# Attention and a rational feed-forward block on one core: a shared step one place later, one normalisation and one block moved, two transfers cut in two

## The chip, the cores and the metric

The kernel runs on one NeuronCore of a Trainium2 chip. The metric is the device time of one execution in microseconds (us). Engines are named as in the profile: PE is TensorE (matmuls; PEld its weight loads), DVE is VectorE, ACT is ScalarE, POOL is GpSimd, SP is the engine that issues nearly all transfers here.

## The reference, cut to what matters

Attention over 4 batches, 8 heads, 576 positions and 64 dimensions, with a bias made by a small network from the distance of two positions, followed by a feed-forward block whose activation is a quotient of polynomials:

```python
scores = (q @ k.T) / 8 + bias            # bias[h,i,j] = relu(x*w1 + b1) @ w2
                                         # x = log1p(|i-j|) / log1p(max(i,1))
attn   = softmax(scores); x = attn @ v   # x: 2304 tokens x 512
h = x @ w_in                             # 512 -> 2048
P = a0 + a1*h + a2*h^2 + a3*h^3
Q = 1 + |b0|*|h| + |b1|*h^2
out = (P / (Q + 1e-6)) @ w_out           # 2048 -> 512
```

All is float32; the feed-forward matmuls are split into a high and a low part (three products for one).

## The kernel before, in words

**Three stages.** First a table of the bias is made, in 36 blocks of 16 rows (lines 688 to 788). For each block four `relu` rows are made on DVE or ACT (line 725), PE multiplies them by the small weights (line 761), ACT scales the result into a tile `e` (line 767), and SP writes it to a table in DRAM (line 772), from which bias tiles are read back (`load_bias`, line 252). Then comes attention, 72 steps taken two at a time in rounds (`rnd`, line 590). Then the feed-forward block, in two passes of 20 steps each (lines 954 to 1001).

**Steps of attention.** A unit `u` is a pair of heads and a batch; there are 16. A unit has 576 rows of scores: four steps of 128 rows (`c` = 0 to 3), and 64 rows that are left. The remainders of units `u` and `u+1` go together as one shared step, written `(u, 4)` with `u` even. Two units make a group of nine steps (`steps`, lines 321 to 323): `(u,0) ... (u,4), (u+1,0) ... (u+1,3)`. Nine is odd and a round takes two steps, so in even groups the shared step is the first of its round, and in odd groups the second. An ordinary step's scores are made with weights in tiles of 64 by 128, a shared step's with tiles of 64 by 64 (line 341); the transposes of line 425 use 64 by 128 and the products with `v` (line 484) 128 by 64.

**A round.** On PE: the scores of steps `i` and `i+1`, the transposes of the probabilities of `i-2` and `i-1`, the products with `v` of `i-3` and `i-2`. On DVE: the bias and the row minimum (`e_ttr`, line 357), copies out of PSUM, and a part of the conversion of the feed-forward weights. On ACT: the exponentials (line 373) and the copies of the transposes (line 440).

**The division by the row sums.** When a unit's last step has been transposed, its sums go through DRAM: `put_tails` writes them (`rs<-rt`, line 462), and `load_rb` (line 386) reads them back, spread over the partitions, with four transfers (`rb<-rs`, lines 392 and 396). `e_norm` (line 401) multiplies the unit's output by them, on POOL (line 408; for unit 12 and the last on DVE), and its result is stored (line 410). Where these are placed is written out in `done_to` (line 530): `load_rb(2g)` at place `7 - g % 2` of group `g`, the normalisation of unit `2g` after the first step of the next group. `rnd` puts at most one normalisation into a round, in a free place of POOL: in the slot `pool`, or in `pool2`.

**The weights.** A job of conversion takes its weights through three rounds (`job_plan`, line 560): POOL copies the middle bits (`wm<-wx`, line 177), DVE joins them (line 181, list `between`), POOL subtracts (line 188, slot `pool2`). In the rounds 11, 20 and 29 the slot `pool` is free: there POOL runs the normalisation of units 2, 6 and 10, then that round's subtraction, then the next round's `wm` copy, for which DVE's join of the next round waits.

**SP's queue.** SP issues in the written order, and an issue that waits holds all behind it. Its issues of a round of the code go out about two rounds of PE later here. The order that the rounds 26 and 27 give is now: the six pieces of a bias load, `rs` of unit 10, `ws<-wl`, `wx` (weights for round 29), `ws<-wh`, `rb` of unit 10 (four), `v`, `q`, `k`, `xr` (the first load of tokens), `ws<-wl`, `wx`. The sizes follow from the tiles: `q` and `k` 288 KB each, `v` 320, `wx` 512, `ws` or `wih`/`woh` 256, this `xr` 576, `rb` 288 in all, `rs` 5.

Of the kernel before, what the change touches and what calls it, by code (L numbers as in the profile page):

```python
# [12 lines left out]
AF = mybir.ActivationFunctionType  # L13
ALU = mybir.AluOpType
# [3 lines left out]
P = 128  # L18
# [3 lines left out]
DM, DFF, NT = 512, 2048, B * S  # L22
# [7 lines left out]
NTT = len(TS)  # L30
# [7 lines left out]
def tile_attn_moe(  # L38
# [194 lines left out]
    with tc.manual_schedule():  # L233
# [3 lines left out]
        with ExitStack() as actx:  # L237
# [82 lines left out]

            steps = [(0, 0), (0, 1), (0, 2), (1, 0), (1, 1), (0, 3), (0, 4), (1, 2), (1, 3)]
            for u in range(2, len(units), 2):
                steps += [(u, c) for c in range(5)] + [(u + 1, c) for c in range(4)]
            s2, prob, pt, tl, xs = {}, {}, {}, {}, {}
            rsum, rb = {}, {}

# [182 lines left out]

            def loads(i):  # L510
                g, c = divmod(i, UPG)
                for u, x, y in ((2 * g + 2, 0 if g else 4, 3 if g else 6), (2 * g + 3, 5 if g else 7, 8)):
                    if u < NU and c == x:
                        load_qk(u)
                    if u < NU and c == y and u != 3:
                        load_v(u)
                if i == UPG + 1:
                    load_v(3)
                p, r = divmod(i, 2 * UPG)
                r = {2: 0, 7: 1, 11: 2, 13: 3, 16: 4}.get(r)  # L520
                if r is not None and p + 1 < NP:
                    load_bias(p + 1, r)
                if i == NS - 18:
                    load_x(0, 0, 0, KD - 1)
                if i == NS - 5:
                    load_x(1, 1, 0, KD - 1)
# [3 lines left out]
            def done_to(k):  # L530
                g, c = divmod(k, UPG)
                u = 2 * g - 2
                if g > 0:
                    if c == (0 if g > 1 else 1) and u != NX or k == NS:
                        norms.extend(e_norm(u))
                    if c == 6 and g * 2 < NU:
                        norms.extend(e_norm(u + 1))
                    if c == 2 and u + 1 < NU - 1:
                        load_rb(u + 1)
                if k == NS - 8:  # L540
                    x12.append(xs[NX])
                    late.extend(e_norm(NX))
                if g < NU // 2 and c == (7 - g % 2 if g else 8):
                    load_rb(2 * g)

            def run(todo):
                while todo:
                    todo.pop(0)()
# [41 lines left out]
            def rnd(r):  # L590
                i = 2 * r
                plan = job_plan(r)
                loads(i)
                op = None
                while puts:
                    op = puts.pop(0)()
                for x in plan["first"]:
                    op = x()
                for x in plan["act"]:
                    x()  # L600
                us = ended(i - 4, i - 3)
                sa, sb = e_qk(i), e_qk(i + 1)
                b, o = side(i), side(i + 1)
                ZZ = (o + 1, o + 3)
                main, ends, adds, copy = e_tp(i - 2, (b, b + 1), ZZ, us)
                main_, ends_, _, copy_ = e_tp(i - 1, (b + 2, b + 3), ZZ)
                weave(sa[0] + sb[0], sa[1] + sb[1])
                for k in ("pool", "pool2"):
                    if not plan[k] and norms:
                        plan[k].append(norms.pop(0))  # L610
                        break
                for x in plan["pool"]:
                    x = x()
                    if op is not None:
                        behind(x, op)
                e_ttr(i, 0, True)
                op = e_ttr(i, 1)
                for x in plan["between"]:
                    op = x()
                for x in plan["pool2"]:  # L620
                    behind(x(), op)
                small = [ends[r] + ends_[r] + adds[r] for r in range(2)]
                weave(main[0][:4] + small[0] + main[0][4:] + main_[0], main[1] + small[1] + main_[1])
                copy(1, 2)
                copy(0, 1)
                copy_(0, 2)
                for j in range(2):
                    e_ttr(i + 1, j)
                put_tails(i - 2, 2, ZZ, us)
                put = e_pv(i - 3, b + 1) if i > 2 else None  # L630
                puts.append(e_pv(i - 2, b))
                hi = split_x(0, (i - NS + 12) // 2) if i in (NS - 12, NS - 10, NS - 8) else ()
                if i == NS - 4:
                    hi = split_x(0, KD - 1, x12[0][:, :TS[0]])
                for x in hi[:1]:
                    x()
                for k in (i, i + 1):
                    for j in range(2):
                        e_exp(k, j)
                recip(i - 2)  # L640
                recip(i - 1)
                if put:
                    put()
                for x in plan["last"] + list(hi[1:]):
                    x()
                done_to(i - 2)
                done_to(i - 1)
                run(late)
                loads(i + 1)
                if r == 2:  # L650
                    for x in jobs[:3]:
                        x[0]()
# [35 lines left out]
            with ExitStack() as bctx:  # L688
# [6 lines left out]
                lts = tpool.tile([P, S], F32, tag="lts", name="lts")  # L695
                bts = tpool.tile([P, NG * 4], F32, tag="bts", name="bts")
                LCUT = 320
                nc.scalar.dma_start(out=cs, in_=cst)
                nc.sync.dma_start(out=lts[:, :LCUT], in_=ltab[:, :LCUT])
                nc.sync.dma_start(out=lts[:, LCUT:], in_=ltab[:, LCUT:])  # L700
                for u in range(2):
                    load_qk(u)
                load_v(0)
                G.memset(qc, 1.0 + 1e-6)
                G.memset(wmin, -8.0 * 0x38000000)
                V.tensor_scalar(out=bts, in0=pts, scalar1=b1s, scalar2=None, op0=ALU.mult)
                A.activation(out=w28, in_=cs[:, 8 + 5 * NG:], func=AF.Identity, scale=8.0)
                for a, z in ((0, LCUT), (LCUT, S)):
                    V.tensor_scalar(
                        out=lts[:, a:z], in0=lts[:, a:z], scalar1=w1s, scalar2=None, op0=ALU.mult  # L710
# [34 lines left out]
                for y, n in enumerate(order):  # L745
                    if y == 13:
                        load_v(1)
                    if y + LEAD < NG:
                        relu(order[y + LEAD])
                    i0 = NROW * n  # L750
                    mid = i0 + NROW - 1
                    pa = 2 * ((y if y >= NG - 2 else y + 2) % 4)
                    pa = (pa, pa + 1)
                    cuts = sorted({0, mid, 512, EW})
                    for a, z in zip(cuts, cuts[1:]):
                        b = pa[a // 512]
                        o = W[:, b, a % 512:a % 512 + z - a]
                        for c in range(4):
                            x = rows[n, c]
                            x = x[:, a - mid:z - mid] if a >= mid else x[:, mid - a:mid - z:-1]  # L760
                            on(T.matmul(  # L761
                                o[32 * c:32 * c + 32], w28[:, 32 * c:32 * c + 32], x,
                                start=True, stop=True,
                            ), b)
                    e = rpool.tile([P, EW], F32, tag="e", name=f"e{n}")
                    o = 512 * pa[0]
                    on(A.activation(  # L767
                        out=e, in_=WF[:, o:o + EW], func=AF.Identity, scale=rts[:, n:n + 1]
                    ), *pa)
                    g, k = divmod(n, 8)  # L770
                    x0 = S - NROW - i0
                    nc.sync.dma_start(
                        out=tab[g][NROW * k:NROW * k + NROW, :, x0:x0 + EW].rearrange("r h x -> (r h) x"),
                        in_=e,
                    )
                    if y in done:
                        load_bias(0, done[y])
                    if y == NG - 1:
                        load_bias(0, 3)
                        load_bias(0, 4)  # L780
                    if y == NG - 3:
                        start(0)
                    if y == NG - 1:
                        start(1)
                        for k in range(2):
                            for j in range(2):
                                e_exp(k, j)
# [19 lines left out]
        with ExitStack() as mctx:  # L807
# [111 lines left out]
            def evac(ready):  # L919
                for n, c in ready:  # L920
# [5 lines left out]
                        part[t, c] = dpool.tile([P, DM], F32, tag=f"pa{t}_{c}", name=f"pa{t}_{c}")  # L926
                        nc.sync.dma_start(out=part[t, c], in_=o)
                    else:
                        o = pre.pop((t, c))
                        on(V.tensor_tensor(out=o, in0=po.pop((n, c)), in1=o, op=ALU.add), OB[c], mem="o")  # L930
                        nc.sync.dma_start(out=out[r0:r0 + P, :], in_=o)

            def load_part(t):
                for c in range(TS[t] // P):
# [145 lines left out]
```

## Time and profile before

| what | us |
|---|---|
| median of 3 runs | 661.66 (660.95 to 662.17) |
| the profiled execution's own time | 662.25 |
| its span, first to last instruction | 660.5 |
| PE busy | 653.5 (99%) |
| DVE busy | 561.3 (85%) |
| ACT busy | 472.2 (71%) |
| POOL busy | 154.1 (23%) |

The table of the bias takes the first 49 us or so, attention lasts to about 265 us, the feed-forward block to the end. Busy shares are of the whole span; a matmul's end is modelled, so PE's rounds are best read from the starts of their first instructions. Rounds are numbered as in the code: round 6 starts at 79.72 us, round 29 at 214.31 us.

### The profile page before, as it was taken

How to read it: one execution, taken by the hardware profiler on the slowest of the kernel's cores; microseconds unless marked ns; L12 is line 12 of the kernel's file. 1: busy time of each engine (PE TensorE's matmuls, PEld its weight loads, DVE VectorE, ACT ScalarE, POOL GpSimd, SP SyncE). 2: the span in 40 equal slices, each digit the busy share in tenths (PEclk: the TensorE clock that was granted, in tenths of full speed). 3: DMA queues.
4: the chain of work that ended last, by engine and by line, in shares of the span. 5: the costliest groups of instructions: out<-in, count | busy, mean ns of one | idle time of the engine just before them, and what ended most of it. 6: DMA issues, size and time to landing. Idle time of an engine off the chain costs nothing.

```text
span 660.5 us, 16193 instructions
## 1 busy us (share of the span) xinstructions
PE 653.5 (99%) x6274; PEld 546.8 (83%) x6274; DVE 561.3 (85%) x1100; ACT 472.2 (71%) x758; POOL 154.1 (23%) x108
## 2 busy tenths in 40 slices
PE   9999999999999999999999999999999999999997
PEld 6657888888888878988888888989988888888996
DVE  7997889988988895899999989979769779687776
ACT  7988999999999987767667566576656555555551
POOL 0000233333433330122212121222221221212211
PEclk9999999999999999999999999999999999999999
DMA  7887878868987975452825607669431301312031
GB/s 242 294 310 226 273 240 266 259 228 231 321 277 226 330 238 167 156 187 72 264 97 164 229 21 249 214 207 318 146 111 49 129 0 65 110 42 86 1 113 48
DMA packets 74845, 118.98 MB, mean 180 GB/s; under 512 B 11904, under 2 KB 33808, under 8 KB 74768
## 3 DMA queue, kind: packets, MB, share of 16 engines
q1 hardware_dynamic: 74624, 117.79, 54.2%
q8 instruction: 49, 0.80, 0.5%
q14 instruction: 28, 0.23, 0.1%
q10 hardware_dynamic: 144, 0.16, 0.1%
HBM read 79.17 MB, written 35.61 MB: 174 GB/s over the span
## 4 chain that ended last, share of the span: by engine, by line
PE 96%; DMA 1%; ACT 1%; issue 1%; DVE 0%; SPq 0%; POOL 0%; DVEq 0%; ACTq 0%; POOLq 0%
PE ps L316 30%; PE ps L909 30%; PE ps L484 12%; PE ps L341 11%; PE ps L761 6%; PE ps L425 6%; DMA tab<-e 1%; DMA bias<-tab 1%; PE ps L713 1%; ACT pt L440 1%; ACT p L373 1%; DVE s L357 0%; SPq L260 0%; DVE pre L930 0%; ACT wh L165 0%
## 5 line engine op out<-in xcount | busy, mean ns | idle before, releaser
L879 POOL TENSOR_TENSOR gl<-m,r 128x1024 fp32r<-128x1024 f32 (+1 forms) x39 | 85.6, 2195 | 295.5 <-DVE m L872 255.7
L830 ACT ACTIVATE w<-ps,babs 128x1024 f32<-128x1024 f32 (+1 forms) x40 | 41.3, 1033 | 107.1 <-PE ps L316 103.4
L373 ACT ACTIVATE p<-s,m 128x576 f32<-128x576 f32 x144 | 110.5, 783 | 0.2 <-DVE m L357 0.2
L357 DVE CUSTOM_DVE_ANT_0 s<-ps,bias 128x576 f32<-128x576 f32 (+1 forms) x144 | 95.2, 682 | 10.1 <-PE ps L341 3.9
L440 ACT COPY pt<-ps 128x512 f32<-128x512 f32 (+1 forms) x109 | 71.9, 732 | 17.6 <-PE ps L425 17.0
L909 PE MATMUL ps<-wol,gh 128*128 128x512 f32 x216 | 84.2, 390 | 0.0
L909 PE MATMUL ps<-woh,gh 128*128 128x512 f32 x216 | 84.2, 390 | 0.0
L341 PE MATMUL ps<-k,q 64*128 64x288 f32 (+1 forms) x640 | 82.3, 418 | 0.4 <-ACT e L767 0.2
L842 DVE SCALAR_TENSOR_TENSOR u<-w,babs,ps 128x1024 f32<-128x1024 f32 (+1 forms) x40 | 46.9, 1172 | 38.1 <-ACT t L831 38.0
L484 PE MATMUL ps<-pt,v 128*64 128x128 f32 (+1 forms) x1280 | 78.2, 265 | 0.8 <-ACT pt L440 0.5
L484 PEld LDWEIGHTS ps<-pt,v 128*64 128x64 f32 x1280 | 65.1, 137 | 5.8 <-ACT pt L440 1.6
L316 PE MATMUL ps<-xb,wih 128*128 128x512 f32 (+1 forms) x240 | 68.8, 367 | 0.0
L341 PEld LDWEIGHTS ps<-k,q 64*128 64x128 f32 (+1 forms) x640 | 50.9, 175 | 20.8 <-issue 6.4
L837 ACT ACTIVATE u<-u 128x1024 f32<-128x1024 f32 (+1 forms) x40 | 39.1, 978 | 40.2 <-DVE u L842 40.0
L425 PEld LDWEIGHTS ps<-ident,p 64*128 64x128 f32 x1296 | 49.6, 138 | 8.7 <-DVE m L357 2.9
L858 DVE SCALAR_TENSOR_TENSOR gh<-t,cst,r 128x1024 fp32r<-128x1024 f32 (+1 forms) x40 | 47.0, 1174 | 9.3 <-ACT r L839 6.9
L909 PE MATMUL ps<-woh,gl 128*128 128x512 f32 x216 | 53.8, 389 | 0.0
L425 PE MATMUL ps<-ident,p 64*128 64x64 f32 x1296 | 51.8, 226 | 0.5 <-ACT p L373 0.2
L865 DVE SCALAR_TENSOR_TENSOR m<-u,qc,gh 128x1024 f32<-128x1024 f32 (+1 forms) x40 | 47.1, 1178 | 4.0
L316 PEld LDWEIGHTS ps<-xb,wih 128*128 128x128 f32 x240 | 44.5, 188 | 6.1
L872 DVE SCALAR_TENSOR_TENSOR m<-t,cst,m 128x1024 f32<-128x1024 f32 (+1 forms) x40 | 47.1, 1179 | 1.4
L851 DVE SCALAR_TENSOR_TENSOR t<-t,cst,ps 128x1024 f32<-128x1024 f32 (+1 forms) x40 | 47.0, 1175 | 1.4
(82 smaller groups left out, 1343.9 us busy)
## 6 DMA issues: line engine op xcount, KB each, us to landing
tab<-e SPq DMA_DIRECT2D x36, 295.5 KB, 3.5
wx<-in_w_in_dram SPq DMA_DIRECT2D x16, 512.0 KB, 5.4
wx<-in_w_out_dram SPq DMA_DIRECT2D x16, 512.0 KB, 4.2
v<-in_vp_dram SPq DMA_DIRECT2D x16, 320.0 KB, 6.3
ws<-wh SPq DMA_DIRECT2D x20, 256.0 KB, 4.7
ws<-wl SPq DMA_DIRECT2D x20, 256.0 KB, 4.3
q<-in_qt_dram SPq DMA_DIRECT2D x16, 288.0 KB, 4.1
k<-in_kt_dram SPq DMA_DIRECT2D x16, 288.0 KB, 3.3
```

The source lines that it names most:

```text
L316: on(T.matmul(hps[s][:, j, :w_], w[:, k, sl], x[:, k, :w_], start=(k == 0 and z == 0), stop=(k == KD - 1 and z == 2),), b + j)
L341: on(T.matmul(W[o, b, :SH], q[r, x], k[r, a * SH:(a + 1) * SH], start=True, stop=True), b)
L357: op = on(V.tensor_tensor_reduce(out=t3[:, a], in0=W[:, b:b + 2][:, a, :SH], in1=b3[:, a], scale=-0.125, scalar=least, op0=ALU.add, op1=AL ...
L373: A.activation(out=prob[i][:, z * S:z * S + S], in_=t, func=AF.Exp, bias=m, scale=-1.0, accum_out=sums[u % 4][:, k:k + 1],)
L425: on(T.transpose(W[:, b, o:o + 64], src[x, :], ident[x, x]), b)
L440: on(A.copy(out=t.rearrange("p x (r s) -> p r x s", r=2)[:, a:z], in_=W[:, to[a]:to[a] + z - a].rearrange("p r (x s) -> p r x s", s=64),), ...
L484: on(T.matmul(ps[y, o], vt[n][:, kc, y], w_, start=(kc == 0), stop=(kc == 4)), b, mem=(f"pt{i % 3}", f"tl{i // 2 % 2}"))
L851: on(V.scalar_tensor_tensor(out=rt[s, "t"], in0=rt[s, "t"], scalar=abs_[:, 1:2], in1=hp(s), op0=ALU.add, op1=ALU.mult,), *hb(s), mem="t")
L865: V.scalar_tensor_tensor(out=m, in0=rt[s, "u"], scalar=qc, in1=rt[s, "gh"].bitcast(F32), op0=ALU.add, op1=ALU.mult,)
L872: V.scalar_tensor_tensor(out=m, in0=rt[s, "t"], scalar=abs_[:, 0:1], in1=m, op0=ALU.add, op1=ALU.subtract)
L879: eng.tensor_tensor(out=lo, in0=rt[s, "m"], in1=rt[s, "r0"], op=ALU.mult)
L909: on(T.matmul(po[n, c], l[:, j, c * P:(c + 1) * P], r[fp][:, j, :], start=(first and x is a), stop=(last and x is z),), OB[c])
```

## The change

The shared step of groups 1, 3 and 5 goes one place later, behind the first step of unit `u+1`, so that it is the first of its round there as well. What hangs on its place moves along: unit `u` ends one step later, so its sums are written one round later (`rs`, by the rule that writes a unit's sums when its last step has been transposed), `load_rb(2g)` in these groups goes one place later, which is one round later, and so does the load of `q` and `k` of unit `2g+3`, from the start to the end of a round. The normalisation of unit `2g` keeps its place. The normalisation of unit 12 goes from the end of round 33 to the middle of round 34, on DVE. The last block of the bias table is scaled on DVE. The constants are loaded in two pieces, the second holding the weights `w2`. The last tile of the output is added and stored in two halves of its columns.

```diff
             for u in range(2, len(units), 2):
-                steps += [(u, c) for c in range(5)] + [(u + 1, c) for c in range(4)]
+                if u % 4 and u + 2 < len(units):
+                    steps += [(u, c) for c in range(4)] + [(u + 1, 0), (u, 4)]
+                    steps += [(u + 1, c) for c in range(1, 4)]
+                else:
+                    steps += [(u, c) for c in range(5)] + [(u + 1, c) for c in range(4)]
...
-                for u, x, y in ((2 * g + 2, 0 if g else 4, 3 if g else 6), (2 * g + 3, 5 if g else 7, 8)):
+                for u, x, y in ((2 * g + 2, 0 if g else 4, 3 if g else 6), (2 * g + 3, 5 + g % 2 if g else 7, 8)):
...
-                if g < NU // 2 and c == (7 - g % 2 if g else 8):
+                if g < NU // 2 and c == (8 if g == 0 else 6 if 2 * g + 2 == NU else 7):
                     load_rb(2 * g)
...
                 for x in plan["between"]:
                     op = x()
+                run(late)
                 for x in plan["pool2"]:
                     behind(x(), op)
...
                 done_to(i - 1)
-                run(late)
                 loads(i + 1)
...
-                nc.scalar.dma_start(out=cs, in_=cst)
+                CCUT = 8 + 5 * NG
+                nc.scalar.dma_start(out=cs[:, :CCUT], in_=cst[:, :CCUT])
                 nc.sync.dma_start(out=lts[:, :LCUT], in_=ltab[:, :LCUT])
                 nc.sync.dma_start(out=lts[:, LCUT:], in_=ltab[:, LCUT:])
+                nc.scalar.dma_start(out=cs[:, CCUT:], in_=cst[:, CCUT:])
...
-                    on(A.activation(
-                        out=e, in_=WF[:, o:o + EW], func=AF.Identity, scale=rts[:, n:n + 1]
-                    ), *pa)
+                    if y < NG - 1:
+                        on(A.activation(
+                            out=e, in_=WF[:, o:o + EW], func=AF.Identity, scale=rts[:, n:n + 1]
+                        ), *pa)
+                    else:
+                        on(V.tensor_scalar(
+                            out=e, in0=WF[:, o:o + EW], scalar1=rts[:, n:n + 1], scalar2=None, op0=ALU.mult
+                        ), *pa)
...
-                        o = pre.pop((t, c))
-                        on(V.tensor_tensor(out=o, in0=po.pop((n, c)), in1=o, op=ALU.add), OB[c], mem="o")
-                        nc.sync.dma_start(out=out[r0:r0 + P, :], in_=o)
+                        o, src = pre.pop((t, c)), po.pop((n, c))
+                        cols = 2 if t == NTT - 1 and c == TS[t] // P - 1 else 1
+                        for h in range(cols):
+                            h = slice(h * DM // cols, (h + 1) * DM // cols)
+                            on(V.tensor_tensor(out=o[:, h], in0=src[:, h], in1=o[:, h], op=ALU.add), OB[c], mem="o")
+                            nc.sync.dma_start(out=out[r0:r0 + P, h], in_=o[:, h])
```

## Rows read from the trace of the kernel before

**Rows 1.** The page, busy time of each engine with its share of the span.

```profile
PE 653.5 (99%) x6274; PEld 546.8 (83%) x6274; DVE 561.3 (85%) x1100; ACT 472.2 (71%) x758; POOL 154.1 (23%) x108
```

**Rows 2.** A stretch of attention: length, busy time per engine, PE's granted clock, DMA share, GB/s.

```profile
100.00:200.00 100.00, 99.89 (x1695) 84.96 (x1693) 89.54 (x308) 93.16 (x200) 37.08 (x30) 1.00 0.82 262
```

**Rows 3.** Timeline of PE, rounds 6 and 11: start, length, operation, count.

```profile
79.72 2.37 PE L341 MATMUL ps<-k,q 64*128 64x288 f32 x24
...
85.76 0.51 PE L341 MATMUL ps<-k,q 64*128 64x288 f32 x2
...
109.03 2.37 PE L341 MATMUL ps<-k,q 64*64 64x288 f32 x24
111.23 1.28 PE L425 MATMUL ps<-ident,p 64*128 64x64 f32 x36
...
114.90 0.51 PE L341 MATMUL ps<-k,q 64*128 64x288 f32 x2
```

**Rows 4.** Timeline of SP, rounds 25 to 28: start and length of each issue.

```profile
192.97 0.33 SPq L462 DMA_DIRECT2D rs<-rt  x1
...
198.46 0.45 SPq L392 DMA_DIRECT2D rb<-rs  x1
210.23 0.47 SPq L462 DMA_DIRECT2D rs<-rt  x1
...
211.19 0.41 SPq L140 DMA_DIRECT2D wx<-in_w_out_dram  x1
...
212.20 0.45 SPq L392 DMA_DIRECT2D rb<-rs  x1
...
213.99 0.60 SPq L396 DMA_DIRECT2D rb<-rs  x1
```

**Rows 5.** Stretches again, for the GB/s of a full DMA queue.

```profile
192.00:199.00 7.00, 7.00 (x107) 5.88 (x105) 6.34 (x23) 6.85 (x17) 2.42 (x2) 1.00 0.98 356
...
211.00:226.00 15.00, 14.81 (x271) 12.52 (x269) 13.32 (x44) 13.39 (x29) 6.84 (x5) 1.00 0.93 285
```

**Rows 6.** Timeline of POOL, rounds 11, 29 and 30; in brackets idle time and releaser.

```profile
109.90 1.42 POOL L408 TENSOR_TENSOR xs<-xs,rb 128x576 f32<-128x576 f32 x1 [2.46 <-DVE wk L156]
...
218.76 1.42 POOL L408 TENSOR_TENSOR xs<-xs,rb 128x576 f32<-128x576 f32 x1 [6.05 <-DMA q<-in_qt_dram]
220.13 1.73 POOL L188 TENSOR_TENSOR wl<-wm,wh 128x512 fp32r<-128x512 f32 x1
221.93 1.04 POOL L177 COPY wm<-wx 128x1024 uint16<-128x1024 uint16 x1
```

**Rows 7.** Timeline of DVE, round 30: the join that reads POOL's copy.

```profile
223.25 0.69 DVE L181 SCALAR_TENSOR_TENSOR wm<-wm,wh 128x512 uint32<-128x512 uint32 x1
```

**Rows 8.** Timeline of SP, then of POOL, rounds 19 to 21.

```profile
156.67 0.35 SPq L140 DMA_DIRECT2D wx<-in_w_out_dram  x1
...
164.54 1.69 POOL L408 TENSOR_TENSOR xs<-xs,rb 128x576 f32<-128x576 f32 x1 [4.48 <-DMA rb<-rs]
...
168.34 1.04 POOL L177 COPY wm<-wx 128x1024 uint16<-128x1024 uint16 x1 [0.87 <-POOL wil L188]
```

**Rows 9.** Timeline of DVE, then of PE's weight loads, start of round 34.

```profile
244.69 0.76 DVE L408 TENSOR_TENSOR xs<-xs,rb 128x576 f32<-128x576 f32 x1 [0.88 <-DMA rb<-rs]
...
245.70 0.79 PEld L341 LDWEIGHTS ps<-k,q 64*128 64x128 f32 x8 [0.59 <-DVE xs L493]
```

**Rows 10.** Waits: engine, line, releaser; total, times, longest.

```profile
DVE bts L706 <- DMA cst<-in_cst_dram: 3.8, 1, 3.8
...
DVE wk L156 <- DMA wx<-in_w_out_dram: 0.6, 1, 0.6
```

**Rows 11.** The chain that ended last, end of the table's stage.

```profile
49.74 4.63 DMA tab<-e
```

**Rows 12.** Timeline at the end: the last addition on DVE.

```profile
656.88 0.69 DVE L930 TENSOR_TENSOR pre<-ps,pre 128x512 f32<-128x512 f32 x1 [0.57 <-PE ps L909]
```

More of the change, by code (lines that the diff above doesn't have):

```diff
@@ L706, in tile_attn_moe @@
                 V.tensor_scalar(out=bts, in0=pts, scalar1=b1s, scalar2=None, op0=ALU.mult)
-                A.activation(out=w28, in_=cs[:, 8 + 5 * NG:], func=AF.Identity, scale=8.0)
+                A.activation(out=w28, in_=cs[:, CCUT:], func=AF.Identity, scale=8.0)
                 for a, z in ((0, LCUT), (LCUT, S)):
```

## The prediction

> **What bounds the kernel now.** I read the profile page's busy shares first: PE is busy for 99% of the span [rows 1]. [...] So a change gains time only where PE's own work gets shorter or one of its few waits goes, and whatever reaches PE late is added in full. The third view is the timelines: a plain round takes 114.90 - 109.03 = 5.87 us [rows 3], so PE needs its operands in that beat. The profiled execution took 662.25 us, 0.59 above the median of 661.66. I make the sum against the first and forecast the second with the same difference.
>
> **The shared step: what PE saves.** Round 6, with a shared step in second place, took 85.76 - 79.72 = 6.04 us, round 11 took 5.87 [rows 3]: 0.17 more. Round 6 also transposes the sums of units, two more transposes than the 36 of round 11; 36 take 1.28 us [rows 3], two 0.07. That leaves 0.10 for one more switch between tiles of 64 by 128 and of 64 by 64, since with the shared step first the order of shapes is that of even groups. Three rounds (6, 15, 24): **-0.3**. Bounds: 0, if the 0.17 has another cause, and -0.5, if all of it goes.
>
> **The shared step: what it moves.** Every issue that hangs on it counts. `qk` of unit 2g+3 goes from the start to the end of a round, several rounds ahead of its use: 0, covered by that distance. `rs` of unit 2g and its four `rb` transfers go one round later on SP; the normalisation on POOL stays. For unit 10, `rs` now stands behind `ws`, `wx`, `ws`, `v`, `q`, `k` and `xr`, and `rb` behind one more `ws` and `wx`.
>
> Before, `rs` was issued at 210.23, the first `rb` at 212.20, the last until 213.99 + 0.60 = 214.59 [rows 4], and POOL began the normalisation at 218.76, after 6.05 us without work [rows 6]: it waited for `rb`, 4.17 us after the last issue. The row names the load of `q` as releaser, which the normalisation does not read; `rb` was queued just ahead of it. Behind the normalisation POOL works without a gap: subtraction at 220.13, copy `wm` from 221.93 to 222.97 [rows 6]. DVE's join, which reads `wm`, starts at 223.25 [rows 7]. So the normalisation may be late by **0.28**. Anything more stops DVE's queue, where the minima and the copies that PE's next round needs stand behind the join; I allow no further slack.
>
> How late is it after? Issues go out every 0.5 us (211.19 and 212.20 are two apart [rows 4]). Without `rs`, the seven loads take 210.23 to 213.7; `rs` follows. Queued ahead of it are 256 + 512 + 256 + 320 + 288 + 288 + 576 = 2,496 KB, 2.56 MB. A full queue moved 285 to 356 GB/s [rows 5], so these take 7.2 to 9.0 us; from 211 they are in at 218.2 to 220.0. A small `rs` behind a full queue was slow before: 5.5 us from its issue to the first `rb` (192.97 to 198.46), against 2.0 in a slack moment (210.23 to 212.20) [rows 4]. SP waits there, with `rb` and the next round's issues behind it. Then four `rb` issues, 2.4, and the landing, 2.0 (as the slack `rs`) to 4.17 (as this `rb` before). The latest case is 220.0 + 2.4 + 4.17 = 226.6. The earliest, with `rs` not held by the bytes ahead, is 213.7 + 2.0 + 2.4 + 2.0 = 220.1. I take 219.1 + 2.4 + 2.0 = 223.5, because this stretch is like the one at 192 us, with a DMA share of 0.93 against 0.98 [rows 5]. 223.5 - 218.76 = 4.7 late, less 0.28: **+4.4**, between +1.0 and +7.5. PE stops for that long in round 30. In round 29 DVE waits 0.6 for `wx` [rows 10]; that load goes one issue earlier without `rs` ahead, but PE then reaches the same stall sooner, so nothing is gained.
>
> [...]
>
> Unit 6: before, POOL normalised at 164.54, and its `wm` copy at 168.34 stood after 0.87 of idle time [rows 8]; with the 0.28 the slack is 1.15. `wx` went out at 156.67 [rows 8]; with `woh`, `v`, `q` and `k` 1,664 KB, 1.70 MB, stand ahead of `rs`, 4.8 to 6.0 us, from 157.7 until 162.5 to 163.7. With 2.4 and 2.0 `rb` lands at 167.5 in the middle, 3.0 late: **+1.8**, between 0 and +4.6 (landing 4.17). Unit 2: POOL was not held by `rb` (its 2.46 of idle time ended with DVE [rows 6]), so there is room of unknown size in front; I take 0, up to +1.8 as for unit 6.
>
> **The normalisation of unit 12.** Before it stood at the start of round 34: DVE waited 0.88 for `rb`, worked 0.76, and PE's weight loads, for which DVE's copies stood behind it, waited 0.59 [rows 9]. In its new place `rb` has long landed and DVE has no join in that round, which covers the 0.76. PE loses about half of the 0.59, as its matmuls trail the loads: **-0.3**, between 0 and -0.6.
>
> **Constants in two pieces.** DVE's first operation waits 3.8 us for `cst` [rows 10]. Of its 158 KB (by the columns of the tile) 64 come later: 0.2 us at 356 GB/s [rows 5], of which I take **-0.1**. Bounds: -0.4, and +0.3 if the second piece holds the first product up. **The last block on DVE**: its store is the link of the chain, 4.63 us from 49.74 [rows 11]; the issue order and that flight stay. 0, within 0.3 either way. **The last output in halves**: the addition takes 0.69 [rows 12]; half of it, 0.35, could overlap the first half's store, less one more issue: **-0.15**, between -0.35 and +0.3. The split of the copies on DVE changes no operation.
>
> **Sum.** 4.4 + 1.8 - 0.3 - 0.3 - 0.1 - 0.15 = +5.35. 662.25 + 5.35 = 667.6, on the median **667.0 us**.
>
> **Rivals.** (a) *The `rb` lands in time* (the other side: faster). If SP's queue drains as early as in the floor for unit 10 and the loads there are small enough to be in by then, no stall remains. The 2.0 us of `rs` in before speaks for it, and the fact that SP issues some two rounds after the code's order, so that its distance to PE can shift; the 5.5 us and the share of 0.93 speak against it. It decides when `rb` lands less than 0.28 us after 218.76. Then only the gains are left, 0.85, and the 0.6 of round 29, of which some 0.35 reaches PE: -1.2, **660.5**. Around it gains between 0.4 and 2 are as likely, so half of this case measures as no change. (b) *A small stall that the gains cancel*: unit 6 holds, unit 10 at its floor of 1.0: 1.0 - 0.85 = +0.15, **661.8**. [...]
>
> **How the numbers follow.** Forecast (a stall of 1.5 us or more) 0.57, with a range of its own of 663.2 to 671; rival (a) 0.33, of which 0.17 is faster by over 0.2% and 0.16 within; (b) 0.05, within; (c) 0.05, slower. 0.2%, 1.3 us, is about what a measurement of this kernel can tell from no change. Faster 0.17; same 0.16 + 0.05 = 0.21; slower 0.57 + 0.05 = 0.62. The range must reach from the gains' lower side, 660.2, over (b) to 671.0.
>
> **What would show it.** Right: in the new profile the last `rb` of unit 10 is issued near 221.5 by the old clock, POOL idles longer than 6.05 ahead of its normalisation, DVE's join shows an idle time with POOL's `wm` as releaser, and round 30 is some 4 us longer than 5.87, round 21 some 2. Rounds 6, 15 and 24 are 0.1 shorter than the 6.04; the weight loads in round 34 no longer wait 0.59. Wrong: `rs` issued to landed in about 2 us in spite of the loads ahead; no wait on `wm`; or a time under 662.

## The result and the profile after

| | us |
|---|---|
| before, median of 6 runs | 661.91 (660.95 to 663.06) |
| changed, median of 6 runs | 670.51 (668.43 to 672.91) |
| ratio, 95% interval | 1.0129 (1.0105 to 1.0153) |
| the profiled execution of the changed kernel | 671.18, span 669.4 |

The changed kernel is slower by 8.6 us; forecast were 5.35 more, 667.0, with a range up to 671.0. The feed-forward block takes the same time in both. The loss is in five of attention's rounds: PE's round 12 is 0.91 us longer than before, round 21 1.97, round 30 5.91, round 31 1.70, round 26 0.33. That is 10.8 in all; other rounds, shorter than before, take back some 1.9 of it.

The timeline of PE (start, length, operation; in brackets idle time and what ended it), rounds 21 and 30 to 32; before, these rounds took 5.9:

```profile
167.53 2.21 PE L345 MATMUL ps<-k,q 64*128 64x288 f32 x16
...
174.52 0.34 PE L488 MATMUL ps<-tl,v 128*64 128x64 f32 x4 [1.75 <-DVE tl L456]
...
175.36 1.00 PE L345 MATMUL ps<-k,q 64*128 64x288 f32 x6
...
222.32 2.21 PE L345 MATMUL ps<-k,q 64*128 64x288 f32 x16
...
226.92 0.64 PE L488 MATMUL ps<-pt,v 128*64 128x64 f32 x16
232.62 0.48 PE L488 MATMUL ps<-tl,v 128*64 128x64 f32 x4 [5.06 <-DVE tl L456]
...
234.09 4.05 PE L345 MATMUL ps<-k,q 64*128 64x288 f32 x16
...
241.66 1.73 PE L345 MATMUL ps<-k,q 64*128 64x288 f32 x12
```

Round 30 (222.32 to 234.09) holds one idle time of 5.06, ended by a copy on DVE. In round 31 the same sixteen matmuls for the scores take 4.05 instead of 2.21. The next view says why. Stretches of the changed kernel: length, busy time of PE, PEld, DVE, ACT and POOL, granted clock, DMA share, GB/s:

```profile
222.32:228.00 5.68, 5.24 (x90) 4.49 (x88) 1.96 (x7) 4.90 (x11) 1.46 (x2) 1.00 0.44 151
228.00:232.60 4.60, 0.00 (x0) 0.00 (x0) 2.29 (x7) 1.88 (x7) 3.49 (x3) 0.83 0.93 231
232.60:234.09 1.49, 1.48 (x24) 1.36 (x24) 1.07 (x5) 0.80 (x3) 0.00 (x0) 0.50 0.71 274
234.09:238.00 3.91, 3.91 (x20) 2.80 (x20) 2.36 (x9) 0.72 (x1) 1.04 (x1) 0.52 1.05 365
238.00:241.66 3.66, 3.66 (x80) 3.36 (x77) 2.94 (x11) 2.97 (x6) 0.00 (x0) 1.00 0.98 325
```

While PE stood, the granted clock fell to 0.50, at 231.0, 3.5 us after the end of PE's last matmul, and it was back at 1.00 at 237.8, after 5.2 us of work. Half of the 1.49 us in round 30, an estimate from the 0.50, and the 1.70 of round 31 are its price: 2.4. So the stall proper is 5.1 and the clock 2.4. Behind the idle time of 1.75 in round 21 the clock stayed at 1.00 (172 to 178 us).

Now back along the chain. DVE, timeline: the join in the rounds 12, 21 and 30; the row of before is [rows 7], without a wait:

```profile
117.77 0.69 DVE L181 SCALAR_TENSOR_TENSOR wm<-wm,wh 128x512 uint32<-128x512 uint32 x1 [0.93 <-POOL wm L177]
...
172.21 0.69 DVE L181 SCALAR_TENSOR_TENSOR wm<-wm,wh 128x512 uint32<-128x512 uint32 x1 [1.98 <-POOL wm L177]
...
230.31 0.69 DVE L181 SCALAR_TENSOR_TENSOR wm<-wm,wh 128x512 uint32<-128x512 uint32 x1 [5.29 <-POOL wm L177]
```

POOL, timeline, as [rows 6, 8]: the normalisations of units 2, 6 and 10 and what follows the last:

```profile
113.89 1.52 POOL L412 TENSOR_TENSOR xs<-xs,rb 128x576 f32<-128x576 f32 x1 [7.22 <-DMA rb<-rs]
...
168.44 1.41 POOL L412 TENSOR_TENSOR xs<-xs,rb 128x576 f32<-128x576 f32 x1 [8.37 <-DMA rb<-rs]
...
226.54 1.41 POOL L412 TENSOR_TENSOR xs<-xs,rb 128x576 f32<-128x576 f32 x1 [11.68 <-DMA rb<-rs]
227.92 1.26 POOL L188 TENSOR_TENSOR wl<-wm,wh 128x512 fp32r<-128x512 f32 x1
229.24 1.04 POOL L177 COPY wm<-wx 128x1024 uint16<-128x1024 uint16 x1
```

All three wait for `rb`, and the last goes without a gap from 226.54 over 229.24 + 1.04 to the join at 230.31. SP, timeline, as [rows 4]:

```profile
212.92 0.38 SPq L273 DMA_DIRECT2D v<-in_vp_dram  x1
...
215.10 0.37 SPq L466 DMA_DIRECT2D rs<-rt  x1
...
216.12 0.33 SPq L140 DMA_DIRECT2D wx<-in_w_in_dram  x1
222.01 0.45 SPq L396 DMA_DIRECT2D rb<-rs  x1
...
223.78 0.59 SPq L400 DMA_DIRECT2D rb<-rs  x1
```

From `rs` issued to the first `rb` 6.9 us pass, against 1.97 before [rows 4]. In this time the DMA engines are fully busy, at a share of 1.01; before, they were at half, 0.48. The stretches of these two waits, changed kernel, then kernel before; the last two numbers are DMA share and GB/s:

```profile
215.00:222.00 7.00, 6.95 (x124) 5.86 (x122) 6.59 (x23) 6.75 (x16) 0.00 (x0) 1.00 1.01 391
```

```profile
210.23:212.20 1.97, 1.97 (x48) 1.66 (x46) 1.87 (x7) 1.81 (x5) 1.16 (x2) 1.00 0.48 153
```

The chain that ended last, which before went over no `rs` at all, holds this very transfer:

```profile
215.10 6.84 DMA rs<-rt
...
223.78 2.60 DMA rb<-rs
```

The sums themselves were not late. DVE's timeline has them ready, 10 rows for unit 10, five us before SP issued `rs`:

```profile
209.83 0.33 DVE L465 COPY rt<-ps 10x64 f32<-10x64 f32 x2
```

### The profile page after: what moved, and what is told of

The parts are those of the page before. It is cut to its first block, busy times and chain, and to the rows that moved or that the text cites. A ratio compares the mean times of both kernels' runs of the same rounds, so it can differ in the third digit from the quotient of the medians.

```text
span 669.4 us, 16201 instructions
## 1 busy us (share of the span) xinstructions
PE 654.9 (98%) x6274; PEld 549.3 (82%) x6274; DVE 561.6 (84%) x1102; ACT 470.9 (70%) x757; POOL 153.4 (23%) x108
## 4 chain that ended last, share of the span: by engine, by line
PE 88%; DMA 4%; ACT 2%; issue 2%; POOL 1%; DVE 1%; SPq 1%; DVEq 0%; POOLq 0%; ACTq 0%
PE ps L316 30%; PE ps L920 29%; PE ps L488 10%; PE ps L345 9%; PE ps L767 6%; PE ps L429 4%; DMA rs<-rt 2%; DMA rb<-rs 1%; ACT p L377 1%; ACT pt L444 1%; DVE s L361 1%; PE ps L719 1%; SPq L396 0%; POOL wm L177 0%; SPq L400 0%
## 5 line engine op out<-in xcount | busy, mean ns | idle before, releaser
L345 PE MATMUL ps<-k,q 64*128 64x288 f32 (+1 forms) x640 | 83.9, 424 | 0.3 <-DVE e L778 0.3
```

Source lines behind the costliest of these rows:

```text
L345: on(T.matmul(W[o, b, :SH], q[r, x], k[r, a * SH:(a + 1) * SH], start=True, stop=True), b)
```

## The experiments

Two theories of the loss. **Queue theory**: `rs` and `rb` are late because they stand behind more bytes, and they hurt through POOL's written order. **Rivals**: the sums are made later; or another edit carries the loss; or the new order of shapes.

**The four small edits alone** (`no_move`).

```diff
-                if u % 4 and u + 2 < len(units):
-                    ...
-                else:
-                    steps += [(u, c) for c in range(5)] + [(u + 1, c) for c in range(4)]
+                steps += [(u, c) for c in range(5)] + [(u + 1, c) for c in range(4)]
...
-                for u, x, y in ((2 * g + 2, 0 if g else 4, 3 if g else 6), (2 * g + 3, 5 + g % 2 if g else 7, 8)):
+                for u, x, y in ((2 * g + 2, 0 if g else 4, 3 if g else 6), (2 * g + 3, 5 if g else 7, 8)):
...
-                if g < NU // 2 and c == (8 if g == 0 else 6 if 2 * g + 2 == NU else 7):
+                if g < NU // 2 and c == (7 - g % 2 if g else 8):
                     load_rb(2 * g)
```

> The changed kernel with the shared step, its loads and its rb transfers at their old places; the other four edits stay. Queue theory (the loss is rs and rb of units 2, 6 and 10 standing later in SP's queue, behind 1.7 to 2.6 MB, so that POOL's normalisation and DVE's join are late): rounds 12, 21 and 30 are back at 5.87 us, round 31 too, round 34 stays at 5.8 instead of 6.14; the time is 0.3 to 0.9 below the kernel before, about 661.2. Rival (one of the other edits carries part of the loss): 663 or more. Round 29 shows the 0.45 of waiting for wx again under both.

Measured: 662.27, ratio 1.0020 (1.0006 to 1.0034); rounds 12, 21, 30 and 31 are back at 5.87. Round 29's 0.45, expected under both, is absent. So at most a small part of the 8.6 us is in these edits. The 0.2%, 1.3 us, is neither expectation. It wasn't in the profiled execution (660.62) and did not come back below, where each edit stands alone and where all stand together in `repaired`; its cause stays open.

**The move alone** (`move_only`): the kernel before with the reverse of that diff, of `steps`, `qk` and `rb` only.

> The kernel before with only the shared step moved, and what hangs on it. Queue theory: rounds 12, 21 and 30 grow by 0.9, 2.0 and 5.9 us, round 31 by 1.7 at a granted clock below 1.00, round 29 loses 0.45 and each of rounds 6, 15 and 24 with the round behind it 0.15: 9 to 10 us slower than before, about 671.4. Rival: a loss under 6.

Measured: 669.66, ratio 1.0117 (1.0094 to 1.0139); rounds 12, 21, 30 and 31 grow by 0.04, 1.79, 5.54 and 1.90. The move is the loss. Round 12's share is not firm: between 0 and 0.9 from one execution to the next.

**Only `rs` and `rb` late** (`rs_late`): the kernel before, its steps as they were; `held` is issued one round on.

```diff
-                    nc.sync.dma_start(out=rsum[u], in_=rt[0:n])
+                    go = lambda u=u, rt=rt, n=n: nc.sync.dma_start(out=rsum[u], in_=rt[0:n])
+                    if u in (2, 6, 10):
+                        held.append(go)
+                    else:
+                        go()
...
+                old, held[:] = list(held), []
                 put_tails(i - 2, 2, ZZ, us)
+                run(old)
...
-                if g < NU // 2 and c == (7 - g % 2 if g else 8):
+                if g < NU // 2 and c == (8 if g == 0 else 6 if 2 * g + 2 == NU else 7):
                     load_rb(2 * g)
```

> The kernel before with its old order of steps, in which only rs and rb of units 2, 6 and 10 are issued one round later on SP, as in the changed kernel; the row sums are ready a round before. If the place in SP's queue behind the loads is the cause: rounds 12, 21, 30 and 31 grow as in move_only, without the 0.15 for each shared step: about 670, 669 to 671. Rival (the sums themselves, or the new order of shapes, make the stall): 661 to 662.

Measured: 671.40, ratio 1.0136 (1.0103 to 1.0170). The timelines of SP and of POOL in this kernel:

```profile
214.10 0.43 SPq L462 DMA_DIRECT2D rs<-rt  x1
...
219.95 0.45 SPq L392 DMA_DIRECT2D rb<-rs  x1
```

```profile
224.60 1.42 POOL L408 TENSOR_TENSOR xs<-xs,rb 128x576 f32<-128x576 f32 x1 [10.79 <-DMA rb<-rs]
```

Here nothing on PE, DVE or ACT was moved, and the sums of unit 10 lay ready as early as before the change; yet rounds 12, 21, 30 and 31 grow by 0.91, 0.91, 5.02 and 2.20. The place of these issues in SP's queue is the cause, not the sums' time and not the shapes.

**Fewer bytes ahead** (`x_behind`), the changed kernel:

```diff
-                if i == NS - 18:
+                if i == NS - 17:
                     load_x(0, 0, 0, KD - 1)
```

> The changed kernel with the first load of tokens (xr, 576 KB) issued behind rb of unit 10 instead of ahead of its rs. Queue theory: 0.59 MB less ahead of rs, at 356 GB/s 1.7 us: the time from rs issued to the first rb falls from 6.9 to about 5.2, round 30 grows by 4.2 instead of 5.9; the clock may stay up then, which is 1.7 more: 667 to 669. Rival (rs is late because the row sums themselves are made one round later, whatever is queued): from rs to rb as before, 670.5.

Measured: 668.08, ratio 1.0107 (1.0086 to 1.0127). SP:

```profile
213.04 0.32 SPq L466 DMA_DIRECT2D rs<-rt  x1
...
217.65 0.45 SPq L396 DMA_DIRECT2D rb<-rs  x1
...
220.43 0.59 SPq L287 DMA_DIRECT2D xr<-xd  x1
```

From `rs` to `rb` 4.6 us instead of 6.9; round 30 grows by 3.09 instead of 5.91, round 31 by 1.27. The wait follows the bytes, by somewhat more than the 1.7 expected. The clock did not stay up: PE's idle time in round 30 is 2.65, and from 230 to 232 us the granted clock is 0.50; the mean of the profiled execution is 0.997, against 0.999 before.

**`rs` on another queue** (`rs_act`), the changed kernel:

```diff
-                    nc.sync.dma_start(out=rsum[u], in_=rt[0:n])
+                    eng = nc.scalar if u in (2, 6, 10) else nc.sync
+                    eng.dma_start(out=rsum[u], in_=rt[0:n])
```

> The changed kernel with the row sums of units 2, 6 and 10 (three transfers of 5 KB) issued by ACT, on its own queue, instead of SP; everything else of the changed kernel stays, the data are ready at the same time. Queue theory (rs waits behind the bytes queued on SP): rs lands about 2 us after its issue although the loads are still under way, SP does not stand before the first rb of these units, which is issued near 217.5 instead of 222.0, and only rb's own bytes and those ahead of it are left: round 30 grows by 0 to 3 us instead of 5.9, round 21 by 0 to 1. 661 to 665. Rival (rs and rb are late because the sums are made a round later, or all transfers share the same engines, so that another queue helps nothing): rb as late as before, 668 to 671.

Measured: 670.90, ratio 1.0159 (1.0133 to 1.0185): a miss, in two ways. The timeline of ACT and that of SP:

```profile
214.05 0.28 ACTq L467 DMA_DIRECT2D rs<-rt  x1
214.38 0.77 ACT L377 ACTIVATE p<-s,m 128x576 f32<-128x576 f32 x1 [5.52 <-DMA wx<-in_w_out_dram]
```

```profile
213.47 0.44 SPq L140 DMA_DIRECT2D wx<-in_w_in_dram  x1
218.80 0.45 SPq L396 DMA_DIRECT2D rb<-rs  x1
```

First, ACT stood for 5.5 us at its own issue, with the exponentials behind it, and round 28 took 13.31. The profile names the landing of a weight load, which the issue does not read; the sums lay ready at 209.4, and why the issue waits for that load is open. The rounds 10 and 19, with ACT's issues for units 2 and 6, are longer by 0.96 and 0.69. The rounds 12, 21, 30 and 31 are back at 5.87: nearly the whole loss of this kernel lies at ACT's issues. Second, alone on ACT's queue `rs` still took 4.75 us (214.05 to 218.80) while SP's loads were under way, at a DMA share of 1.02 to 1.07. So the order within SP's queue is not needed for a late `rs`: while the DMA engines are this busy, it is late on another queue too. With round 28 disturbed this is one reading, not a clean size. That `rs` waits for all bytes queued ahead of it, as the +4.4 has it, was the author's estimate; by the 4.75 us the order within SP's queue is not the whole reason here, and what held `rs` on ACT's queue is not shown.

**POOL's order** (`norm_later`), the changed kernel:

```diff
-                    if c == (0 if g > 1 else 1) and u != NX or k == NS:
+                    if c == (1 if g == 1 else 2 if g in (2, 4, 6) else 0) and u != NX or k == NS:
```

> The changed kernel with the normalisation of units 2, 6 and 10 two rounds later on POOL (rounds 13, 22 and 31, slot pool2). rs and rb stay as late as they are. Queue theory, in which the late rb hurts only through POOL's order (normalisation, subtraction, wm copy, DVE's join): the stalls of rounds 12, 21 and 30 go, the fall of the clock in round 31 with them, the gains stay: 662 - 0.45 - 0.45 - 0.34 = 660.7, less up to 0.5 at the start. Rival (SP stands up to 7 us on its wait for rs, and the loads behind it are late as well): DVE waits for wx or PE for v or q instead, rounds 30 to 33 grow by 2 us or more, 663 to 668.

Measured: 664.20, ratio 1.0042 (1.0024 to 1.0060), single executions from 661.11 to 668.17. In the profiled one (661.11) rounds 12, 21, 30 and 31 are back at 5.87, so the path over POOL is the one that hurt. But the rival holds as well: SP still stands before `rb`, up to 4.7 us, round 29 takes 6.68, and most executions lose more. `move_norm_x` shows where.

**The same, with the tokens behind** (`move_norm_x`): `move_only` with the edits of `norm_later` and `x_behind`.

> The kernel before with the shared step moved, the normalisations of units 2, 6 and 10 two rounds later and the first load of tokens behind rb of unit 10; the four small edits are left out. The move's own gain is 3 x 0.15 = 0.45, and there is room of two rounds for rb: 660.5, ratio 0.9993. Rival (SP still stands 4 to 5 us before rb in each of the three places, so that loads behind it are late in some executions, as the spread of norm_later suggests): median 662 to 663, some executions above 665.

Measured: 666.47, ratio 1.0062 (1.0041 to 1.0083). SP, then DVE:

```profile
213.47 0.33 SPq L140 DMA_DIRECT2D wx<-in_w_out_dram  x1
...
217.67 0.31 SPq L466 DMA_DIRECT2D rs<-rt  x1
```

```profile
218.96 0.43 DVE L156 TENSOR_SCALAR wk<-wx 128x512 uint32<-128x512 uint32 x1 [3.98 <-DMA wx<-in_w_out_dram]
```

The stall has moved: the weights that SP issued at 213.47 (211.19 before [rows 4]) land too late for DVE, by 3.98 us, and round 29 takes 11.99. It is the wait of 0.6 in [rows 10], grown. That SP issued them later because it had stood before `rb` of earlier units is argued; the next run, with `rb` of these units a round later, is the test.

**SP does not stand** (`move_norm_rb`): `move_only` with the edit of `norm_later`, and `rb` one round after `rs`.

```diff
-                if g < NU // 2 and c == (8 if g == 0 else 6 if 2 * g + 2 == NU else 7):
+                if g < NU // 2 and g not in (1, 3, 5) and c == (8 if g == 0 else 6 if 2 * g + 2 == NU else 7):
                     load_rb(2 * g)
+                if g in (2, 4, 6) and c == 0:
+                    load_rb(2 * g - 2)
```

> As move_norm_x, but the tokens are loaded at their old place, and rb of the three units is issued one round after its rs instead of right behind it, so that SP does not stand waiting for rs. If SP's wait is what spread norm_later: 660.5 with a spread like before's, ratio 0.9993. Rival (rb then lands too near to the normalisation, or the load of tokens ahead still delays what follows): 662 or more.

Measured: 661.51, ratio 1.0000 (0.9986 to 1.0014), 660.71 to 663.9: the loss is gone, and the spread is like before's.

**The small edits one by one** (`start_only`, `norm12_only`, `halves_only`): the kernel before with the diff's parts for the constants and the last block, for the normalisation of unit 12, and for the last output.

> The kernel before with the constants in two pieces and the last block scaled on DVE, nothing else. If the four small edits of no_move together cost the 0.2% and this pair is the cause: 662 to 663, 0.15 to 0.3% above before. If they are only worth the half us that PE's start showed in the changed kernel: 660.5, 0.05 to 0.1% below before. The first product on PE is at 5.57 us in both traces so far, so the start's half us may be the clock of that execution and not the edit.

> The kernel before with the normalisation of unit 12 between the passes of round 34, nothing else. By the traces so far round 34 takes 5.79 instead of 6.14: 0.3 us faster, ratio 0.9995. If this edit is what makes no_move 0.2% slower (DVE and ACT's copy of the tokens wait in the middle of a round for an rb that is late in some executions): ratio above 1.0015, with a wide spread.

> The kernel before with the last output tile added and stored in two halves, nothing else. The traces so far show 3.66 us from PE's end to the end of the span in both forms: no change, ratio 0.9995 to 1.0005. If the second small store is what makes no_move 0.2% slower: ratio above 1.0015, and a span that ends later after PE's last matmul.

Measured: ratios 0.9999 (0.9990 to 1.0008), 0.9998 (0.9987 to 1.0009) and 0.9999 (0.9990 to 1.0008). None does anything that can be told. The traces say why. In `halves_only`, where the normalisation of unit 12 stands at its old place, DVE and the weight loads of round 34 read

```profile
242.87 0.73 DVE L408 TENSOR_TENSOR xs<-xs,rb 128x576 f32<-128x576 f32 x1
```

```profile
243.46 1.76 PEld L341 LDWEIGHTS ps<-k,q 64*128 64x128 f32 x16 [0.17 <-issue]
```

without the waits of 0.88 and 0.59 in [rows 9]: those belonged to that one execution, in which `rb` was late; round 34 takes 5.79 or 5.80 in all thirteen other profiles. The same holds for 0.38 in round 2. Round 29's extra 0.45 comes and goes: it is in neither `start_only` nor `halves_only`, but the profiled executions of `norm12_only` and `norm_later` have 0.58 and 0.81 there. The profiled execution of before took 662.25, where most runs of before take 660.5 to 661.5.

**All of the change, repaired** (`repaired`): the changed kernel with the edits of `norm_later` and `move_norm_rb`.

> The whole changed kernel with the two repairs of move_norm_rb (normalisation of units 2, 6 and 10 two rounds later, their rb one round after their rs). If the late rs and rb are all of the loss and the four small edits are worth nothing together, as each was alone: 661.4, ratio 1.000, within 0.15%. Rival (the four small edits together cost the 0.2% that no_move showed): ratio 1.002, with single executions at 665.

Measured: 660.70 (660.38 to 661.53, 11 runs) against 661.45, ratio 0.9986 (0.9976 to 0.9996). SP, then POOL:

```profile
207.30 0.60 SPq L466 DMA_DIRECT2D rs<-rt  x1
...
212.52 0.28 SPq L466 DMA_DIRECT2D rs<-rt  x1
...
214.66 0.45 SPq L396 DMA_DIRECT2D rb<-rs  x1
```

```profile
226.06 1.04 POOL L177 COPY wm<-wx 128x1024 uint16<-128x1024 uint16 x1 [2.12 <-issue]
227.93 1.42 POOL L412 TENSOR_TENSOR xs<-xs,rb 128x576 f32<-128x576 f32 x1 [0.83 <-DVE m L361]
```

The first `rs` shown is unit 10's, the second unit 11's. `rb` goes out 7.4 us after its `rs` and 13 us ahead of the normalisation, which waits for DVE alone and stands behind the copy, not ahead of it. By the two ratios this version is some 9.5 us below the changed one. From `norm_later`, at 1.0042, it differs by the later `rb` alone. It is also 0.75 below before, with an interval that just leaves out 1. The rounds 6, 15 and 24 and those behind them give some 0.45 of that; `move_norm_rb`, with the same order of steps, measured 1.0000, so how much of the 0.75 is the change's is not shown.

## Why the prediction was right, and where its sizes were off

The direction, the mechanism and each of its links are as put: `rs` behind the loads, `rb` late, POOL's three instructions without a gap, the join, PE. The time lies in the range, 0.5 below its upper end, and that is in part luck: unit 2's 0.9 and the clock's 2.4 stood at 0 in the sum. By its steps, profiled execution against profiled execution:

| step | forecast | measured | from |
|---|---|---|---|
| shapes, three rounds | -0.3 | -0.5 | rounds 6, 15, 24: -0.23 each, the rounds behind them +0.08 |
| stall of unit 10 | +4.4 | +5.1 | PE idle 5.06 in round 30 |
| stall of unit 6 | +1.8 | +2.0 | round 21 |
| stall of unit 2 | 0 | +0.9 | round 12 (0.04 in `move_only`) |
| clock | 0 | +2.4 | granted clock 0.50 |
| unit 12, start, last output | -0.55 | 0 | the three runs of single edits |

The measured column sums to 9.9. Rounds 4 and 26 add 0.5, and 1.6 go off for time that the profiled execution of before lost and this one did not (0.78 up to round 3, 0.45 in round 29, 0.34 in round 34): 8.8, against 669.4 - 660.5 = 8.9. Of the 0.78, 0.40 is in the start of round 2, which lies between 55.1 and 55.9 us in the fourteen profiles, with the edit of the constants and without.

- **The main term** was under-sized by 0.7. `rs` to the first `rb` took 6.9, where I had 5.4 (213.7 to 219.1); `rs` itself went out 0.75 earlier against the start of round 28; from the first `rb` to the normalisation it was 4.5, forecast 2.4 + 2.0. At 391 GB/s some 2.7 MB went by in the 6.9 us. That is more than was left of the 2.56 MB ahead of `rs`, so the 0.79 MB issued behind it may well have gone ahead of its landing too; no run tells the two apart. Nor does a run show the +4.4, or the +1.8 of unit 6, as they were made up, by an `rs` that waits for all bytes queued ahead of it: the runs show 6.9 us from `rs` to the first `rb`, 4.6 with 0.59 MB less ahead (`x_behind`) and 4.75 on ACT's queue (`rs_act`).
- **Unit 2** was given room of unknown size from a row that named DVE; it had almost none in this execution, and enough in another.
- **The clock** is the step that failed. I set its fall against the forecast, as rival (c) with a chance of 0.05; it is no other way than the forecast but a consequence of it: behind PE's idle time in round 30 the granted clock was 0.50 in the changed kernel (5.06), `move_only` (4.69), `rs_late` (4.16) and `x_behind` (2.65). The means of these profiled executions are 0.994, 0.994, 0.994 and 0.997, against 0.999 before. In `rs_act` it was 0.50 too, from 217 to 221 us, after 3.75 us of idle time in round 28. With a price of 2.4 the sum gives 667.0 + 2.4 = 669.4, but the price could not be read from the rows of before: the clock is 1.00 there [rows 2, 5], and PE never idle that long.
- **The small gains** were read from waits of one execution and taken as those of the kernel.
- Round 29's 0.45, said to be given back at the next stall, most likely was: `rs` of unit 10 went out at 215.10, before round 29 began at 216.44, so an earlier PE could not end the stall earlier.
- Round 26 takes 0.33 more in six of the eight kernels with the move and in none without it; no run here tells its cause.

## What to carry to other kernels

When a step moves later, follow its transfers and not only its arithmetic: what they stand behind in the queue, what is waited for in order behind their arrival, and how much slack the consumer has (0.28 us here). If a small transfer must be followed by another that depends on it, put a round between their issues and move the consumer later as well, here by two rounds; that gave back some 9.5 us. Before a wait in a profile is counted as a gain, look whether a second execution has it too. And a stall of PE can cost the clock behind it: here 2.4 us on top of 5.1, at a granted clock of 0.50.

## What was not expected of the hardware

From the issue of a transfer of 5 KB to the next issue that waits for it, 6.9 us passed with the DMA engines at a share of 1.01, and 1.97 at a share of 0.48. On another engine's queue, at a share of 1.02 to 1.07, it was 4.75: a queue of its own did not make it quick. ACT stood 5.5 us at its issue of it; the profile names the landing of a load that the issue does not read.
